# Three small first reads on ACT's queue, transposes of x in another order, and a new order of work in a gated mix of attention and a gated MLP

## The chip, the cores and the metric

The kernel runs on one core of a Trainium2 chip. The metric is the time of one execution on the device, in microseconds (us). TensorE (PE) multiplies matrices, VectorE (DVE), ScalarE (ACT) and GpSimd (POOL) do the rest, and SyncE (SP) issues the DMAs.

## The reference

The input x has 2048 tokens of 512 elements in bf16. Two branches are computed from it and mixed by a gate per token.

```python
x = A_x
g = _sigmoid((x * gate_w).sum(-1, keepdims=True))
a = _A_ref(x, A_wq, A_wk, A_wv, A_wo, A_beta)     # attention
b = _B_ref(x, B_W_gate, B_W_up, B_W_down)         # gated MLP, F = 1792
return g * a + (1 - g) * b
```

`_A_ref` has 32 heads of 16 elements and cuts the tokens into 4 segments of 512. Within a segment it is causal softmax attention. Beside it, each segment reads a memory `M` (with its norm `z`) that sums `phi(k) v` over the segments before, and a gate per head mixes the two. `_B_ref` is `(relu(x Wg) * (x Wu)) Wd`.

## The kernel before, in words

Everything is held in SBUF. A segment passes through these stages: projections to q, k and v (lines 770 to 814), scores in 18 "visits" (`att`, L872; the score matmuls are L904), the exponential of a visit in one pass over four PSUM banks by ACT (L920), masks of the diagonal by POOL (L926), the product with V (L960), a read-out of the memory (L847), an update of the memory (L827), the MLP's first half by 14 column blocks (L1034, with relu on ACT or DVE at L1042 and L1043, and the product with the up branch on DVE at L1045), and its second half together with the output projection (L1066, L1073). Results go through `osb` to DRAM (L1085).

The first segment's x is read in two halves into `hT` (L627) and transposed by PE against an identity (L700) into four PSUM banks, in two halves h and four quarters kt. DVE and ACT copy the results into `xT` in turns (L705). The weights follow on SP's queue in the order of the calls of `load`: wq, wk, wv, the first halves of the gate (wg) and up (wu) weights, the gate vector, beta (`braw`), and the second halves (L617). The x of later segments is read by transposing DMAs (L619). ek, from which the memory is updated, is transposed by DMA too (`phik`, L807). Rows of x for the token gate go through `osb` (L734, L737).

The order of the work isn't written by hand. `Sched` (L129) is a planner that runs while the program is built: each operation has a cost in ns, what it reads and writes, and a queue with a priority. Step by step the planner takes the operation that can start first (`_choose`, L462), gives it a PSUM bank, and appends it to its engine's list with the semaphore waits that it needs (`_waits`, L359). It has tables of how long DMAs take (`DCOST`, L35, and `LAND0`, L36). Where several operations are ready, random numbers decide; their seeds are listed by stretches of 8 us (L565). Thus a change of a cost or a seed at one place shifts the order of everything behind it. At the end SP waits for each DMA's semaphore (L1157).

The waits for several semaphores are sorted by name:

```python
for st, idx in sorted(deps.items(), key=lambda kv: (kv[0] == e, kv[0])):
```

Of the kernel before, what the change touches and what calls it, by code (L numbers as in the profile page):

```python
# [8 lines left out]
ACT = mybir.ActivationFunctionType  # L9
ALU = mybir.AluOpType  # L10
# [21 lines left out]
X2_T = 34000.0  # L32
H1_T = 14000.0
LX = 300.0
DCOST = {"ldbraw": 1800.0, "ldgwb": 1300.0, "ldx1_0": 1500.0, "vsh0": 1100.0, "vsh1": 1100.0, "vsh2": 1100.0, "vsh3": 1100.0}  # L35
# [8 lines left out]
ADP = 1  # L44
# [84 lines left out]
class Sched:  # L129
# [3 lines left out]
    def __init__(self, ndma=16, nbanks=8, seeds=(0,)):  # L133
        self.seeds = seeds
        self.jit = {}
        self.knobs = {}
        self.low_from = False
        self.mates = ()
        self.bank_ep = [None] * nbanks
        self.ndma = ndma  # L140
        self.streams = list(self.ENGS) + [f"dma{i}" for i in range(ndma)]
        self.cnt = {s: 0 for s in self.streams}
        self.know = {e: {s: 0 for s in self.streams} for e in self.ENGS}
        self.snap = {s: {0: {t: 0 for t in self.streams}} for s in self.streams}
# [12 lines left out]
        self.prog = {e: [] for e in self.ENGS}  # L157
        self.busy = {e: 0.0 for e in self.ENGS}
        self.ops = []
        self.log = []  # L160
        self.sem = {}
# [207 lines left out]

    def place(self, op, e, start):  # L370
        op.eng = e
        if op.ep is not None and op.role == "w" and op.ep.bank is None:
            got = self._banks(op, e)[0]
            for ep, bi in zip([g[0] for g in got], sorted(g[1] for g in got) if op.ep.cls == "main" else [g[1] for g in got]):
                for i in range(bi, bi + ep.nb):
                    if self.bank_ep[i] is not None:
                        op.preds += [(r, False) for r in self.bank_ep[i].readers]
                    self.bank_ep[i] = ep
                ep.bank = bi
        if e == "pool" and self.yield_to is not None:  # L380
            op.preds.append((self.yield_to, False))
            self.yield_to = None
        deps = {}
        for p in self._pred_done(op, e):
            deps[p.stream] = max(deps.get(p.stream, 0), p.idx)
        self._waits(e, deps)
        occ = op.occs[e]
        op.base = occ
        if e == "dve" and op.port:
            if self.pool_from <= start < self.now["pool"]:  # L390
                occ += self.now["pool"] - start
                self.yield_to = op
            self.port_free = start + occ
        if e == "pool":
            if start > self.now["pool"] + 1.0:
                self.pool_from = start
        if e == "pe":
            if op.mode != self.mode or start > self.now[e] + 60.0:
                occ += SWITCH
            self.mode = op.mode  # L400
        if op.dma:
            d = min(range(self.ndma), key=lambda i: (self.dma_end.get(i, 0.0), i))
            st = f"dma{d}"
            if self.cnt[st] > 0:
                self._waits(e, {st: self.cnt[st]})
            self.cnt[st] += 1
            self.semval[st, self.cnt[st]] = self.semval.get((st, self.cnt[st] - 1), 0) + 16 * op.nd
            inc = 16
            issued = start + occ
            op.end = max(self.dma_busy + self.dcost(op) if op.nbytes > 4096 and op.name not in LAND0 else 0.0, start + self.landing(op, start) + (0.0 if op.name in LAND0 else LX))  # L410
            self.dma_busy = max(self.dma_busy, op.end) if op.nbytes > 4096 else self.dma_busy
            self.dma_end[d] = op.end
        else:
            st = e
            self.cnt[st] += 1
            inc = 1
# [12 lines left out]
        self.busy[e] += occ  # L429
        self.log.append((start, start + occ, e, op.name))  # L430
# [128 lines left out]
def build_kernel(nc, A_x, A_wq, A_wk, A_wv, A_wo, A_beta, W_g, W_u, W_d, gate_w, out):  # L559
# [5 lines left out]
    sc = Sched(seeds=(140892, 423927, 0, 0, 0, 892626, 168011, 223314, 641091, 969207, 0, 695128, 872014, 0, 136527, 629242, 695393, 450067, 491946, 378858, 0, 909379, 857173, 62279, 0, 744487, 417792, 0,))  # L565
    T = {}
    with contextlib.ExitStack() as stack:
        for name, shape, dt in plan(S, D, F):
# [10 lines left out]
def program(sc, nc, T, PS, A_x, A_wq, A_wk, A_wv, A_wo, A_beta, W_g, W_u, W_d, gate_w, out, NSEG, KT, NF, NT, EPS, SCALE):  # L579
# [19 lines left out]
    def act(fn, occ, **k):  # L599
        return op("act", fn, occ, **k)  # L600
# [41 lines left out]
    load("sp", ["braw"], V.braw[:], A_beta.partition_broadcast(128), 8192)  # L642
    load_gu(1)
    lact.insert(0, act(lambda e: e.activation(V.eb[:, 0:8], nc.const_aps.tensor(1.0, [128, 8], BF16), ACT.Exp), 1450, writes=["eb"], name="tab"))
    sc.queue(0, lact)
    sc.queue(0, lsp)
    lsp = []
# [17 lines left out]
    st = []  # L665
# [25 lines left out]
        return pe(fn, m * n * (0.834 if k == 0 else 0.5), writes=[f"bankL{b}"], name=f"warm{k}")  # L691

    xps, xcs = [warm(5, 512, 0, 3), warm(6, 128, 0, 3)], {"dve": [], "act": []}
    for h in range(2):
        for kt in range(KT):
            eng = ("dve", "act")[kt % 2]

            def fx(e, h=h, kt=kt):
                for i in range(2):
                    ins = e.matmul(PL[:, kt, 128 * i:128 * i + 128], lhsT=V.hT[:, 2 * h + i, kt * 128:(kt + 1) * 128], rhs=V.ident[:], start=True, stop=True)  # L700
                return ins
            xps.append(pe(fx, 205, reads=[f"hT{2 * h}", "ident"], writes=[f"bankL{kt}"], name=f"xt{4 * h + kt}"))
            src = PL[:, kt, 0:256].rearrange("q (i t) -> q t i", i=2)
            dst = V.xT[:, kt, h * 256:(h + 1) * 256].rearrange("q (t i) -> q t i", i=2)
            cpy = (lambda e, d=dst, x=src: e.tensor_copy(d, x)) if eng == "dve" else (lambda e, d=dst, x=src: e.activation(d, x, ACT.Copy))  # L705
            xcs[eng].append(op(eng, cpy, 440 if eng == "dve" else 400, reads=[f"bankL{kt}"], writes=[f"xT0_{kt + 4 * h}"], name=f"xc{4 * h + kt}"))
    sc.queue(0, xps)
    sc.queue(0, xcs["dve"])
    sc.queue(0, xcs["act"])
# [162 lines left out]
    def att(s, between):  # L872
# [57 lines left out]
        def flush():  # L930
# [52 lines left out]
            ds.append((dve if s == NSEG - 1 or not ADP else pool)(lambda e: e.tensor_tensor(av, Tv[:, :, :, 0:16], gv.unsqueeze(3).to_broadcast([128, 2, 16, 16]), ALU.mult), 690 if s == NSEG - 1 or not ADP else 1100, reads=tn + [f"rdg{G % 2}"], writes=["adT"], name=f"ad{s}_{G}"))  # L983
# [210 lines left out]
```

## Time and profile before

| what | us |
|---|---|
| runs | 265.81, 265.82, 266.25 (median 265.82) |
| profiled execution, own time | 266.2 |
| its span in the trace | 264.5 |
| mean granted clock of PE | 0.999 |

The profile is of one execution. The page gives each engine's busy time as a share of the span, then the span in 40 slices with the busy share in tenths, and the chain of work that ended last. The other views group instructions by line, list who waited for whom, or list instructions in order of time; "x4" is the count that was merged into a row, and the bracket at the end of a row is the idle time before it and what ended it. "PEld" is the load of weights into PE, which overlaps its matmuls. "SPq" is SP issuing a DMA; its duration is that of the issue, not of the transfer. Numbers such as L904 are lines of the kernel before; in the kernel after the same line stands 2 to 9 lines further down.

### The profile page before, as it was taken

What the parts mean: (1) busy time and instruction counts of PE and PEld (TensorE: products, weight loads), DVE (VectorE), ACT (ScalarE), POOL (GpSimd) and SP (SyncE); (2) the same over time, 40 slices, a digit from 0 to 9 for tenths busy, and PEclk for the clock granted to TensorE, in tenths of its full rate; (3) what the DMA queues carried; (4) which work ended last, traced back from release to release, by engine and by line L of the source; (5) the groups of instructions that cost most, each with busy time, mean ns of one, the idle gap of its engine ahead of it and who ended that gap; (6) DMA issues with size and microseconds to landing.
All of it is one profiled execution on the core that took longest, in us unless ns stands there. A gap on an engine that the chain in (4) does not pass through costs nothing.

```text
span 264.5 us, 6437 instructions
## 1 busy us (share of the span) xinstructions
PE 255.7 (97%) x2618; PEld 114.0 (43%) x2653; DVE 179.8 (68%) x355; ACT 185.5 (70%) x161; POOL 130.8 (49%) x295
## 2 busy tenths in 40 slices
PE   8899999999999999999999999999999999999996
PEld 4333443434444444434443544434444444344444
DVE  5378597888788494688788775776664676557600
ACT  4577688987788877876868676886786565676021
POOL 3026565645655464865556375756464454544000
PEclk9999999999999999999999999999999999999999
DMA  6889744912550223210141112500132100000011
GB/s 203 268 318 225 147 100 89 296 38 56 85 126 9 58 60 85 59 22 2 40 107 41 42 40 44 62 19 4 33 89 64 42 0 22 21 2 0 2 42 40
DMA packets 34829, 19.87 MB, mean 75 GB/s; under 512 B 23920, under 2 KB 34032, under 8 KB 34800
## 3 DMA queue, kind: packets, MB, share of 16 engines
q1 hardware_dynamic: 34800, 19.46, 30.2%
q8 instruction: 21, 0.34, 0.5%
q14 instruction: 8, 0.07, 0.1%
HBM read 10.40 MB, written 2.11 MB: 47 GB/s over the span
## 4 chain that ended last, share of the span: by engine, by line
PE 91%; SPq 3%; DMA 2%; issue 2%; DVE 1%; DVEq 0%
PE ps L1034 37%; PE ps L1073 19%; PE ps L904 9%; PE ps L784 8%; PE ps L960 7%; PE ps L782 5%; PE ps L1066 5%; SPq L617 3%; DMA wu<-in_B_W_up_dram 2%; PE ps L847 1%; PE ps L827 0%; DVE Tn L970 0%; DVE qT L793 0%; DVE oT L986 0%; DVE osb L1082 0%
## 5 line engine op out<-in xcount | busy, mean ns | idle before, releaser
L926 POOL TENSOR_SCALAR_AFFINE_SELECT E<-E 64x256 bf16<-64x256 bf16 (+1 forms) x256 | 111.0, 444 | 109.6 <-ACT E L920 83.9
L920 ACT ACTIVATE E<-ps 128x2048 bf16<-128x2048 f32 x72 | 135.0, 1875 | 36.8 <-PE ps L904 36.3
L1034 PE MATMUL ps<-xT,wg 128*128 128x512 bf16 x215 | 58.1, 380 | 2.4 <-DMA wg<-in_B_W_gate_dram 1.4
L1034 PE MATMUL ps<-xT,wu 128*128 128x512 bf16 x215 | 57.2, 380 | 1.3 <-issue 1.0
L1073 PE MATMUL ps<-wd,hT 128*128 128x512 bf16 (+2 forms) x229 | 54.0, 367 | 1.1 <-issue 0.9
L1045 DVE TENSOR_TENSOR hT<-ps,rl 128x512 bf16<-128x512 f32 x56 | 38.4, 686 | 19.4 <-PE ps L1034 19.0
L1034 PEld LDWEIGHTS ps<-xT,wg 128*128 128x128 bf16 x224 | 20.3, 98 | 27.7 <-issue 3.9
L1034 PEld LDWEIGHTS ps<-xT,wu 128*128 128x128 bf16 x224 | 20.1, 98 | 25.9 <-issue 2.7
L1073 PEld LDWEIGHTS ps<-wd,hT 128*128 128x128 bf16 x238 | 21.1, 98 | 23.0 <-issue 2.8
L970 DVE STREAM_TRANSPOSE Tn<-ps 128x512 f32<-128x512 f32 x32 | 21.2, 695 | 13.9 <-PE ps L960 13.9
L904 PE MATMUL ps<-qT,kp 32*128 32x192 bf16 (+7 forms) x512 | 28.6, 287 | 0.0
L1043 DVE TENSOR_SCALAR rl<-ps 128x512 bf16<-128x512 f32 x31 | 21.2, 684 | 5.0 <-PE ps L1034 4.2
L1042 ACT ACTIVATE rl<-ps 128x512 bf16<-128x512 f32 x25 | 14.9, 598 | 13.1 <-PE ps L1034 13.1
L904 PEld LDWEIGHTS ps<-qT,kp 32*128 32x128 bf16 x512 | 8.3, 92 | 25.5 <-issue 13.1
L960 PE MATMUL ps<-E,vaug 64*17 64x128 bf16 (+7 forms) x512 | 18.7, 284 | 0.0
L960 PE MATMUL ps<-E,vsh 64*17 64x128 bf16 (+7 forms) x512 | 18.3, 283 | 0.0
L1083 ACT ACTIVATE osb<-ps,omg 128x512 bf16<-128x512 f32 (+1 forms) x9 | 6.1, 675 | 16.9 <-PE ps L1066 14.0
L784 PE MATMUL ps<-xT,wq 128*128 128x512 bf16 x64 | 16.5, 380 | 0.1
L1082 DVE TENSOR_SCALAR osb<-ps,omg 128x512 bf16<-128x512 f32 (+1 forms) x8 | 5.6, 699 | 16.0 <-PE ps L1066 11.4
L1066 PE MATMUL ps<-wo,oT 128*128 128x512 bf16 (+2 forms) x66 | 16.4, 367 | 0.1
L784 PE MATMUL ps<-xT,wk 128*128 128x512 bf16 x60 | 15.9, 380 | 0.3 <-issue 0.2
L782 PE MATMUL ps<-wv,xT 128*128 128x512 bf16 x62 | 15.4, 380 | 0.2 <-issue 0.2
(68 smaller groups left out, 229.9 us busy)
## 6 DMA issues: line engine op xcount, KB each, us to landing
vsh<-vaug SPq DMA_DIRECT2D x8, 272.0 KB, 3.7
osb<-in_A_x_dram SPq DMA_DIRECT2D x16, 128.0 KB, 2.3
out_dram<-osb SPq DMA_DIRECT2D x15, 128.0 KB, 1.7
wg<-in_B_W_gate_dram SPq DMA_DIRECT2D x8, 224.0 KB, 5.9
wu<-in_B_W_up_dram SPq DMA_DIRECT2D x8, 224.0 KB, 6.1
wd<-in_B_W_down_dram SPq DMA_DIRECT2D x1, 1792.0 KB, 10.3
hT<-in_A_x_dram SPq DMA_DIRECT2D x2, 256.0 KB, 3.0
wq<-in_A_wq_dram SPq DMA_DIRECT2D x4, 128.0 KB, 3.0
```

The lines of the kernel that those rows point to most:

```text
L782: ins = e.matmul(A(ep)[:, :], lhsT=V.xT[:, kt, tok + col * 128:tok + (col + 1) * 128], rhs=w[:, kt, :], start=(kt == 0), stop=(kt == KT - 1))
L784: ins = e.matmul(A(ep)[:, :], lhsT=w[:, kt, col * 128:(col + 1) * 128], rhs=V.xT[:, kt, tok:tok + 512], start=(kt == 0), stop=(kt == KT - 1))
L904: ins = q.matmul(dst, lhsT=V.kp[r, kslot(s, G), c, :], rhs=V.qT[r, qslot(s, G), q0:q0 + w], start=True, stop=True, tile_position=(32 * jj, ...
L920: acts.append(act(lambda a: a.activation(V.E[:, base * 512:base * 512 + min(2048, 4 * W)], PF[:, 0:min(2048, 4 * W)], ACT.Exp, scale=SCALE ...
L926: pools.append(pool(lambda g, ap=ap, lim=lim, pat=pat: g.affine_select(out=ap, in_=ap, compare_op=ALU.is_ge, fill=0.0, base=lim, pattern=[ ...
L960: ins = q.matmul(A(eps[p])[32 * jj:32 * jj + 17, 64 * (c + u):64 * (c + u + n)], lhsT=v[:, 8 * G + 2 * jj + p, :], rhs=V.E[r, f:f + 64 * n ...
L970: ds.append(dve(lambda e, p=p, ep=eps[p]: e.transpose(V.Tn[:, 2 * (G % (TNN // 2)) + p, :], A(ep)[:, :]), t_dve(512), writes=[f"Tn{2 * (G ...
L1034: ins = e.matmul(A(ep)[:, :], lhsT=w[:, kt, f * 128:(f + 1) * 128], rhs=V.xT[:, kt, c % XR * 512:(c % XR + 1) * 512], start=(kt == 0), sto ...
L1043: ("dve", lambda e, ep=eg, r=r: e.tensor_scalar(V.rl[:, r, :], A(ep)[:, :], 0.0, None, ALU.max), t_dve(512))],
L1045: evs.append(dve(lambda e, ep=eu, r=r, hs=hs: e.tensor_tensor(V.hT[:, hs, :], A(ep)[:, :], V.rl[:, r, :], ALU.mult), t_dve(512), reads=[f" ...
L1066: ins = e.matmul(A(ep)[:, 0:c1 - c0], lhsT=V.oT[:, ot[G], i * 128:(i + 1) * 128], rhs=V.wo[:, G, c0:c1], start=st_ and G == 0, stop=sp_ an ...
L1073: ins = e.matmul(A(ep)[:, 0:c1 - c0], lhsT=V.hT[:, slots[f], i * 128:(i + 1) * 128], rhs=V.wd[:, f, c0:c1], start=st_ and f == f0, stop=sp ...
```

## The change

Three reads of 16 x 32 elements, one each from the gate, up and down weights, are issued on ACT's DMA queue, behind ACT's first exponential (the one that loads its table). They write into `adT`, which holds nothing yet; its first real writer waits for them. No result uses what they read.

The transposes of x have another order, and one of the eight uses a fifth PSUM bank that the planner picks. DVE and ACT still copy four results each, but not the same ones: DVE has (h, kt) = (0,0), (1,0), (0,3), (1,2), ACT has (0,1), (0,2), (1,1), (1,3). Before, DVE had the even quarters and ACT the odd ones, first of h = 0 and then of h = 1.

The planner gets a cost of 1000 ns for the first gate weight's DMA, 10 ns less for each copy of x, and other seeds. With that the whole order of work is planned anew. Waits for several semaphores are listed with the latest first, and so are SP's waits at the end. In the built program PE starts with 16 query matmuls, 14 of the keys, a visit, 2 of the keys, 10 of V, a visit, 6 of V, and then 4 of the gate and 4 of the up weights. Before, the 17th and later matmuls were 10 of the keys, 2 of the gate, 2 of the keys, a visit, and then gate, key, up and V matmuls by turns of two.

```diff
-DCOST = {"ldbraw": 1800.0, ...}
+DCOST = {"ldwg0_0": 1000.0, "ldbraw": 1800.0, ...}
@@ Sched._waits
-        for st, idx in sorted(deps.items(), key=lambda kv: (kv[0] == e, kv[0])):
+        for st, idx in sorted(deps.items(), key=lambda kv: (-self.end_of.get(kv, 0.0), kv[0])):
@@ Sched.place
+        self.end_of[st, idx] = op.end
@@ build_kernel
-    sc = Sched(seeds=(140892, 423927, 0, 0, 0, 892626, ...))
+    sc = Sched(seeds=(237719, 74891, 0, 89398, 0, 53401, ...))
@@ program
     lact.insert(0, act(lambda e: e.activation(V.eb[:, 0:8], ..., ACT.Exp), 1450, writes=["eb"], name="tab"))
+    for n, w in enumerate((W_g, W_u, W_d)):
+        load("act", [f"touch{n}"], V.adT[0:16, 32 * n:32 * n + 32], w[0:16, 0:32], 1024)
...
-    for h in range(2):
-        for kt in range(KT):
-            eng = ("dve", "act")[kt % 2]
+    for h, kt, bank, eng in ((0, 0, 0, "dve"), (0, 1, 1, "act"), (0, 2, 2, "act"), (1, 0, None, "dve"), (0, 3, 3, "dve"), (1, 1, 0, "act"), (1, 2, 1, "dve"), (1, 3, 2, "act")):
+        ep = Epoch("att") if bank is None else None
...
-            xcs[eng].append(op(eng, cpy, 440 if eng == "dve" else 400, ...))
+        xcs[eng].append(op(eng, cpy, 430 if eng == "dve" else 390, ...))
@@ flush, the first writer of adT
-... writes=["adT"], name=f"ad{s}_{G}"))
+... writes=["adT"] + ([f"touch{n}" for n in range(3)] if s + G == 0 else []), name=f"ad{s}_{G}"))
@@ end of program
-    for i in sorted(range(sc.ndma), key=lambda i: sc.dma_end.get(i, 0.0)):
+    for i in sorted(range(sc.ndma), key=lambda i: -sc.dma_end.get(i, 0.0)):
```

More of the change, by code (lines that the diff above doesn't have):

```diff
@@ L34 @@
 LX = 300.0
-DCOST = {"ldbraw": 1800.0, "ldgwb": 1300.0, "ldx1_0": 1500.0, "vsh0": 1100.0, "vsh1": 1100.0, "vsh2": 1100.0, "vsh3": 1100.0}
+DCOST = {"ldwg0_0": 1000.0, "ldbraw": 1800.0, "ldgwb": 1300.0, "ldx1_0": 1500.0, "vsh0": 1100.0, "vsh1": 1100.0, "vsh2": 1100.0, "vsh3": 1100.0}
 LAND0 = {"ldhT0": 2850.0, "ldhT2": 3100.0, "ldwq0": 3150.0, "ldwq1": 3200.0, "ldwq2": 3100.0, "ldwq3": 3000.0}
@@ L157, in __init__ @@
         self.prog = {e: [] for e in self.ENGS}
+        self.end_of = {}
         self.busy = {e: 0.0 for e in self.ENGS}
@@ L564, in build_kernel @@
     EPS, SCALE = 1e-6, 16 ** -0.5
-    sc = Sched(seeds=(140892, 423927, 0, 0, 0, 892626, 168011, 223314, 641091, 969207, 0, 695128, 872014, 0, 136527, 629242, 695393, 450067, 491946, 378858, 0, 909379, 857173, 62279, 0, 744487, 417792, 0,))
+    sc = Sched(seeds=(237719, 74891, 0, 89398, 0, 53401, 416309, 0, 0, 0, 710933, 0, 718714, 120896, 538430, 820480, 585027, 870794, 793690, 0, 589972, 0, 0, 0, 454998, 16783, 0,))
     T = {}
@@ L693, in program, with B, fx, cpy @@
     xps, xcs = [warm(5, 512, 0, 3), warm(6, 128, 0, 3)], {"dve": [], "act": []}
-    for h in range(2):
-        for kt in range(KT):
-            eng = ("dve", "act")[kt % 2]
[L698 to L706, printed above, removed]
+    for h, kt, bank, eng in ((0, 0, 0, "dve"), (0, 1, 1, "act"), (0, 2, 2, "act"), (1, 0, None, "dve"), (0, 3, 3, "dve"), (1, 1, 0, "act"), (1, 2, 1, "dve"), (1, 3, 2, "act")):
+        ep = Epoch("att") if bank is None else None
+        bk = [] if bank is None else [f"bankL{bank}"]
+        def B(ep=ep, bank=bank):
+            return A(ep) if bank is None else PL[:, bank, :]
+        def fx(e, h=h, kt=kt, B=B):
+            for i in range(2):
+                ins = e.matmul(B()[:, 128 * i:128 * i + 128], lhsT=V.hT[:, 2 * h + i, kt * 128:(kt + 1) * 128], rhs=V.ident[:], start=True, stop=True)
+            return ins
+        xps.append(pe(fx, 205, reads=[f"hT{2 * h}", "ident"], writes=bk, name=f"xt{4 * h + kt}", ep=ep, role=ep and "w"))
+        dst = V.xT[:, kt, h * 256:(h + 1) * 256].rearrange("q (t i) -> q t i", i=2)
+        def cpy(e, d=dst, B=B, eng=eng):
+            x = B()[:, 0:256].rearrange("q (i t) -> q t i", i=2)
+            return e.tensor_copy(d, x) if eng == "dve" else e.activation(d, x, ACT.Copy)
+        xcs[eng].append(op(eng, cpy, 430 if eng == "dve" else 390, reads=bk, writes=[f"xT0_{kt + 4 * h}"], name=f"xc{4 * h + kt}", ep=ep, role=ep and "r"))
     sc.queue(0, xps)
@@ L982, in flush @@
             av = V.adT[:, :].rearrange("q (c p e) -> q p c e", p=2, e=16)
-            ds.append((dve if s == NSEG - 1 or not ADP else pool)(lambda e: e.tensor_tensor(av, Tv[:, :, :, 0:16], gv.unsqueeze(3).to_broadcast([128, 2, 16, 16]), ALU.mult), 690 if s == NSEG - 1 or not ADP else 1100, reads=tn + [f"rdg{G % 2}"], writes=["adT"], name=f"ad{s}_{G}"))
+            ds.append((dve if s == NSEG - 1 or not ADP else pool)(lambda e: e.tensor_tensor(av, Tv[:, :, :, 0:16], gv.unsqueeze(3).to_broadcast([128, 2, 16, 16]), ALU.mult), 690 if s == NSEG - 1 or not ADP else 1100, reads=tn + [f"rdg{G % 2}"], writes=["adT"] + ([f"touch{n}" for n in range(3)] if s + G == 0 else []), name=f"ad{s}_{G}"))
             os_ = (s * 4 + G) % OTN
```

## The prediction

> **What bounds the kernel now.** I read the page first: the span, the busy time of TensorE (PE), its row of 40 slices, and the chain that ended last.
>
> ```profile
> span 264.5 us, 6437 instructions
> PE 255.7 (97%) x2618; PEld 114.0 (43%) x2653; DVE 179.8 (68%) x355; ACT 185.5 (70%) x161; POOL 130.8 (49%) x295
> PE   8899999999999999999999999999999999999996
> PE 91%; SPq 3%; DMA 2%; issue 2%; DVE 1%; DVEq 0%
> ```
>
> PE is busy nearly all the time and is 91% of the chain. No other engine passes 70%. The only slices below 9 are the first two and the last. So the second step is the view of busy time in stretches, and the waits of PE.
>
> ```profile
> 5.60:17.40 11.80, 10.19 (x53) 4.00 (x54) 5.72 (x14) 6.47 (x9) 1.34 (x2) 1.00 0.84 276
> 17.50:261.00 243.50, 239.71 (x2527) 106.49 (x2558) 170.25 (x333) 175.71 (x147) 127.11 (x279) 1.00 0.28 63
> PE ps L1034 <- DMA wg<-in_B_W_gate_dram: 1.4, 2, 1.2
> PE ps L1034 <- DMA wu<-in_B_W_up_dram: 0.2, 1, 0.2
> ```
>
> After the length of each stretch, the first number is PE's busy time; 1.00 is the granted clock. From 17.5 us on PE is busy 239.71 of 243.50 us, at full clock, and waits for no transfer. Its only waits for data are in the first stretch: three for the gate and up weights. The third step is the order in time there, and a piece of the middle as a yardstick.
>
> ```profile
> 5.60 3.61 PE L784 MATMUL ps<-xT,wq 128*128 128x512 bf16 x16
> 12.54 0.59 PE L1034 MATMUL ps<-xT,wg 128*128 128x512 bf16 x2 [1.17 <-DMA wg<-in_B_W_gate_dram]
> 13.50 0.39 PE L904 MATMUL ps<-qT,kp 32*128 32x512 bf16 x4
> 14.09 0.59 PE L1034 MATMUL ps<-xT,wg 128*128 128x512 bf16 x2 [0.20 <-DMA wg<-in_B_W_gate_dram]
> 15.31 0.59 PE L1034 MATMUL ps<-xT,wu 128*128 128x512 bf16 x2 [0.19 <-DMA wu<-in_B_W_up_dram]
> 16.60 0.59 PE L1034 MATMUL ps<-xT,wu 128*128 128x512 bf16 x2
> 42.58 0.60 PE L1034 MATMUL ps<-xT,wg 128*128 128x512 bf16 x2
> 43.11 0.40 PE L904 MATMUL ps<-qT,kp 32*128 32x512 bf16 x4
> 43.44 0.61 PE L1034 MATMUL ps<-xT,wg 128*128 128x512 bf16 x2
> 43.88 1.03 PE L1034 MATMUL ps<-xT,wu 128*128 128x512 bf16 x4
> 44.74 1.03 PE L1034 MATMUL ps<-xT,wg 128*128 128x512 bf16 x4
> ```
>
> Starts, not ends, tell PE's pace, since a matmul's recorded length overlaps the next. Four matmuls of 512 columns go from 43.88 to 44.74: **0.216 us each**. A visit to the scores (L904) costs 0.33 us (43.11 to 43.44) and 0.10 to enter it (42.58 plus two steps is 43.01; it starts at 43.11).
>
> With that yardstick the start is measured. Before the first visit stand 30 matmuls of 512 columns (16 for queries, 12 for keys, 2 for the gate): 5.60 + 30 x 0.216 + 0.10 = 12.18. The visit starts at 13.50, so 1.32 us are lost. It ends at 13.83, and the next matmul starts at 14.09: 0.26 lost. Four matmuls later it would be 14.95; the next starts at 15.31: 0.36 lost. Together **1.94 us**, all of it PE waiting for gate and up weights that were put among the keys.
>
> **The change part by part.**
>
> *The order of PE's work.* The instructions of both kernels hold the same work: 946 matmuls of 512 columns or less behind the transposes, 72 visits, 16 products with V, 3 memory updates, 12 read-outs of the memory. PE enters the other kinds of work about as often (78 stretches of plain matmuls against 80, and each visit, product and update follows its kind of neighbour nearly as often), so I put the steady part at no change, 0.0. What moves is the beginning. The new order is 16 query matmuls, 14 of the keys, the first visit, 2 of the keys, 10 of V, the second visit, 6 of V, and only then the gate and up weights. So the 1.94 us of waiting go if what is late next comes in time. Each neighbour by its time, with queries starting at 5.35 (next part): the first visit is due at 5.35 + 6.48 + 0.10 = 11.93. It needs two key tiles copied by ACT and two masks by DVE.
>
> ```profile
> 10.98 0.60 ACT L789 ACTIVATE kT<-ps 128x512 bf16<-128x512 f32 x1 [0.27 <-PE ps L784]
> 11.61 1.06 ACT L766 ACTIVATE ek<-kT 128x1024 bf16<-128x1024 bf16 x1
> 13.94 1.88 ACT L920 ACTIVATE E<-ps 128x2048 bf16<-128x2048 f32 x1 [1.28 <-PE ps L904]
> ```
>
> The second copy ends at 11.58 now, and 0.25 earlier then: 11.33, so 0.6 us of room. The first exponential starts once the visit is through and the 1.06 us pass of ek is done: 12.4 to 14.3. The second visit needs it, and is due at 11.93 + 0.33 + 12 x 0.216 + 0.10 = 14.95: again 0.6. The gate weights are due at 14.95 + 0.33 + 6 x 0.216 = 16.6. The rows above show them landed by 14.09 (both pairs are used by then). The up weights are due at 17.4 and were landed by 16.60. So the whole 1.94 is counted as gained.
>
> *The transposes of x.* Now DVE and ACT copy four results each.
>
> ```profile
> 3.71 1.80 PE L700 MATMUL ps<-ident,hT 128*128 128x128 bf16 x16
> 4.14 1.66 DVE L705 CAST xT<-ps 128x256 bf16<-128x256 f32 x4 [0.98 <-PE ps L700]
> 4.35 1.57 ACT L705 ACTIVATE xT<-ps 128x256 bf16<-128x256 f32 x4 [2.04 <-PE ps L700]
> 5.05 0.46 PE L700 MATMUL ps<-ident,hT 128*128 128x128 bf16 x4
> ```
>
> The first query matmul needs both halves of the first quarter of x. The second half is DVE's third copy: 4.14 + 3 x 0.415 = 5.39, and PE starts at 5.60. In the new order it is DVE's second copy, done by about 5.2. Then the end of the transposes decides. The last one waits for ACT's second copy in both orders (4.35 + 2 x 0.39 = 5.14). Now the last four matmuls start at 5.05 and end at 5.50; at 0.22 each the last starts at 5.28, and a step of 128 columns (a quarter of 0.216) later PE is free: 5.34. So queries start at about 5.35: **0.25 us gained**. From below it is 0, if another copy is late; from above 0.35.
>
> *The three small reads.* ACT issues them after its first exponential and before its copies of x.
>
> ```profile
> 2.10 0.21 ACT L644 ACTIVATE eb<-const-bfloat16-1.0 128x8 f32<-128x8 bf16 x1
> L617 SPq DMA_DIRECT2D wu<-in_B_W_up_dram x8: 430/526/1192, 9.3 to 17.2; - x8
> DMA packets 236, 0.17 MB, mean 145 GB/s; under 512 B 109, under 2 KB 236, under 8 KB 236
> q1 hardware_dynamic: 236, 0.17, 49.4%
> ```
>
> No DMA is issued on ACT now, so its price is bounded by SP's rows: 0.43 to 1.19 us each. ACT is free at 2.31 and needed at 4.35. Three at 0.43 end at 3.6 and cost nothing; three at 1.19 end at 5.9 and delay the start by 1.5. I take 0.43, the usual row while the queue is not full, so 0. What waits behind them on ACT are the copies of x. Their packets are small; the last two rows are the 1.2 us from 15.4 on, when 64-byte packets of another load pass: 236 packets take 49.4% of 16 engines, 40 ns each. Three packets and as many completions per engine are 0.25 us at most for the first query weights, which are not due before 5.35. What the reads may gain is less time for the first gate read; nothing waits for it any more, so 0.
>
> The Trainium skill speaks against these reads (DMA: Bandwidth & Descriptors, "Issuing engines are not separate DMA queues"): DMAs of ACT and SP share 16 engines and interleave, so another issuing engine only saves issue time. By that rule the reads push into the loads of x and query weights; by the 40 ns above that is at most 0.25, and the sum would be 0.25 smaller, an estimate. No run here shows the mix yet.
>
> *Waits listed with the latest first, and the last waits on SP.*
>
> ```profile
> 261.72 1.15 SPq L1085 DMA_DIRECT2D out_dram<-osb  x2
> out_dram<-osb SPq DMA_DIRECT2D x15, 128.0 KB, 1.7
> ```
>
> The last store is issued near 262.5 and lands 1.4 to 1.7 later, so 264.0 to 264.2; the span ends at 264.5. At most 0.5 lies behind the landing. In the built program the wait for that store moves from the second to last place on SP to the last, so one wait less is left behind it. Bounds 0 to 0.4; I take 0, as only one of some ten steps moves. Elsewhere PE, which sets the time, hardly waits, so the order of waits is worth 0 there.
>
> **Sum.** 1.94 + 0.25 = 2.19 us. The profiled execution's own time is 266.2 (span 264.5 and 1.7 around it): 264.0. It stands 0.4 above the median of the runs, 265.82; from that the sum gives **263.65, I say 263.7**.
>
> **The rivals.**
>
> *A. ACT is late.* The three issues take over 0.68 us each (2.04 of room by three), or their packets hold up x. Against it: SP's first issues of 0.43. For it: a queue that has not been used. At 0.9 each the start slips 0.7, at 1.19 by 1.5: 264.3 to 265.2.
>
> *B. Waits come back in small pieces.* The gate and up work starts 4 us later, so DVE meets V copies and key masks together near 14 to 20 us, and a shifted order can put an exponential in front of a visit. One such wait is at most one exponential, 1.88: 264.3 to 265.5. Against it: in the old order nothing of the kind shows in 243.5 us, and visits in the new order are no closer to each other (2.6 us at the least in both, by the prices above).
>
> *C. Slower: x of the second segment is behind on SP.* Now three of its four transposed pieces are issued by 25.4 us, the fourth at 30.54.
>
> ```profile
> 22.97 2.45 SPq L619 DMA_TRANSPOSE xT<-in_A_x_dram  x2
> 26.82 3.68 SPq L807 DMA_TRANSPOSE phik<-ek  x2
> 30.54 1.26 SPq L619 DMA_TRANSPOSE xT<-in_A_x_dram  x1
> 31.85 3.03 SPq L734 DMA_DIRECT2D osb<-in_A_x_dram  x3
> DMA to landing us min/median/max: 2.7/3.1/4.8
> 33.94 1.03 PE L784 MATMUL ps<-xT,wq 128*128 128x512 bf16 x4
> 24.76 0.90 DVE L768 TENSOR_TENSOR ek<-ek,ttmp 128x1024 bf16<-128x1024 bf16 x1
> ```
>
> In the new order three of them stand behind the transposes of ek and two loads of rows of x, one of which waits for a gate pass on DVE. From the second ek pass (done at 25.66 now) I count 2 x 1.26, 2 x 0.6 and 2 x 1.25 until the last issue starts at 31.9; with 2.7 to 3.1 to land (the row of landings) it is in at 34.6 to 35.0. PE wants it at 33.94 - 2.19 + 16 matmuls + one visit = 35.6. So 0.6 to 1.0 of room, and each us beyond it stops PE one for one. To end slower than 266.35 it must be 0.6 + 2.2 + 0.5 = 3.3 us late, one full round of waiting on DVE; then 266.4 to 268.
>
> *D. The reads do not do what they are named for.* If the first gate reads are as slow as now, nothing changes here: 263.7 as well.
>
> **How the numbers follow.** A difference under 0.2% (0.53 us) can't be told from no change here. Forecast, D within it: 0.68, at 263.2 to 264.3. A: 0.12. B: 0.14, a third of it within 0.2%. C: 0.06. Faster (under 265.29): 0.68 + 0.11 + 0.08 = 0.87; same 0.06; slower 0.07. The range goes from 263.2 to 265.0: the forecast with its bounds (start gain 0.35; last waits 0.4), and most of A and B.
>
> **What would show it.** In the changed kernel's timeline the queries start at 5.3 to 5.4; the first visit at 11.9 to 12.0 and the second at 15.0; no wait of PE for the gate or up weights; three issues on ACT that end before 4.3; the query work of segment two near 35.6 with no wait for x; and a span of about 262.3. I am wrong if PE shows gaps between 12 and 40 us, or if ACT's first copy starts after 4.4.

## The result, and the profile after

| | runs | median, us | lowest to highest |
|---|---|---|---|
| before | 6 | 266.13 | 265.81 to 266.30 |
| changed | 6 | 264.32 | 263.60 to 264.61 |

The ratio is 0.9931, with a 95% interval of 0.9915 to 0.9946: 1.81 us faster, where 2.19 were forecast. The forecast of 263.7 started from the median of the first three runs, 265.82; that of all six is 266.13. 264.32 lies at the upper edge of the forecast's own 263.2 to 264.3, and at the lower edge of what rivals A and B were given. The profiled execution of the changed kernel took 264.5 us, 1.7 less than that of the kernel before.

The page of the changed kernel (span, busy time, PE's 40 slices, the chain that ended last):

```profile
span 262.7 us, 6432 instructions
PE 255.7 (97%) x2619; PEld 114.6 (44%) x2653; DVE 179.1 (68%) x356; ACT 184.5 (70%) x160; POOL 131.0 (50%) x295
PE   8999999999999999999999999999999999999996
PE 97%; issue 1%; DVE 1%
```

PE is busy for the same 255.7 us in a shorter span, and the two 8s at the start have become one. DMA and SP are gone from the chain. The waits of PE in the changed kernel, the longest first:

```profile
PE ps L1043 <- issue: 1.6, 10, 0.2
PE ps L693 <- PEq L1188: 0.8, 1, 0.8
PE ps L793 <- issue: 0.6, 4, 0.2
PE ps L1082 <- issue: 0.6, 4, 0.2
PE ps L1043 <- DVE Tn L979: 0.2, 1, 0.2
```

No row names the gate or up weights. (L1043 is the line that was L1034, L793 was L784 and L913 was L904.) The start of the changed kernel in order of time:

```profile
3.69 1.95 PE L707 MATMUL ps<-ident,hT 128*128 128x128 bf16 x16
5.43 4.21 PE L793 MATMUL ps<-xT,wq 128*128 128x512 bf16 x16
9.48 3.19 PE L793 MATMUL ps<-xT,wk 128*128 128x512 bf16 x13
12.60 0.40 PE L913 MATMUL ps<-qT,kp 32*128 32x512 bf16 x4
13.37 2.32 PE L791 MATMUL ps<-wv,xT 128*128 128x512 bf16 x10
15.62 0.40 PE L913 MATMUL ps<-qT,kp 32*128 32x448 bf16 x8
17.26 1.03 PE L1043 MATMUL ps<-xT,wg 128*128 128x512 bf16 x4
```

From the first visit at 12.60 on, the rows follow the prices: the second visit stands 0.33 + 12 x 0.216 + 0.10 = 3.02 later. But the first visit was forecast for 11.93. The second row tells why: 16 query matmuls take 4.21 us where they took 3.61. Up to the first key they take 9.48 - 5.43 = 4.05, against 9.05 - 5.60 = 3.45. The 0.60 more is what about 1.2 us at half the pace cost: until about 6.6 us a matmul took 0.43, then 0.216. The trace also holds a record of the granted clock, and its first entry, at full clock, begins at 6.63. The transposes of x (first row) stand ahead of that and ran at half pace too.

The difference of the spans (264.45 to 262.75 in the trace, 1.71) then splits as follows: the two stretches of waiting 1.32 + 0.60; the earlier start of the queries 0.17; the slow first queries -0.59; steps elsewhere 0.06; the end, behind the last matmul, 0.15.

### The profile page after: what moved, and what is told of

Same layout as the page of the kernel before. It is cut to its first block, busy times and chain, and to the rows that moved or that the text cites. A ratio compares the mean times of both kernels' runs of the same rounds, so it can differ in the third digit from the quotient of the medians.

```text
span 262.7 us, 6432 instructions
## 1 busy us (share of the span) xinstructions
PE 255.7 (97%) x2619; PEld 114.6 (44%) x2653; DVE 179.1 (68%) x356; ACT 184.5 (70%) x160; POOL 131.0 (50%) x295
## 4 chain that ended last, share of the span: by engine, by line
PE 97%; issue 1%; DVE 1%
PE ps L1043 38%; PE ps L1082 19%; PE ps L793 11%; PE ps L913 9%; PE ps L969 6%; PE ps L791 5%; PE ps L1075 5%; PE ps L856 1%; PE ps L693 1%; PE ps L707 1%; PE ps L836 0%; DVE hT L1054 0%; DVE Tn L979 0%; DVE osb L746 0%; DVE osb L1091 0%
## 5 line engine op out<-in xcount | busy, mean ns | idle before, releaser
L1043 PE MATMUL ps<-xT,wu 128*128 128x512 bf16 x213 | 57.2, 380 | 1.4 <-issue 1.3
L1043 PE MATMUL ps<-xT,wg 128*128 128x512 bf16 x219 | 57.7, 380 | 0.6 <-issue 0.3
L1082 PE MATMUL ps<-wd,hT 128*128 128x512 bf16 (+2 forms) x229 | 52.8, 367 | 0.9 <-issue 0.6
L1043 PEld LDWEIGHTS ps<-xT,wg 128*128 128x128 bf16 x224 | 20.6, 98 | 25.7 <-issue 2.8
L1043 PEld LDWEIGHTS ps<-xT,wu 128*128 128x128 bf16 x224 | 20.1, 98 | 25.4 <-issue 3.5
L913 PE MATMUL ps<-qT,kp 32*128 32x192 bf16 (+7 forms) x512 | 28.6, 287 | 0.0
L1051 ACT ACTIVATE rl<-ps 128x512 bf16<-128x512 f32 x26 | 15.5, 598 | 9.9 <-PE ps L1043 9.7
L913 PEld LDWEIGHTS ps<-qT,kp 32*128 32x128 bf16 x512 | 8.2, 92 | 25.3 <-issue 13.1
L793 PE MATMUL ps<-xT,wq 128*128 128x512 bf16 x61 | 16.1, 391 | 0.4 <-issue 0.3
L793 PE MATMUL ps<-xT,wk 128*128 128x512 bf16 x60 | 15.6, 380 | 0.4 <-issue 0.3
```

What stands on the lines that cost most here:

```text
L793: ins = e.matmul(A(ep)[:, :], lhsT=w[:, kt, col * 128:(col + 1) * 128], rhs=V.xT[:, kt, tok:tok + 512], start=(kt == 0), stop=(kt == KT - 1))
L913: ins = q.matmul(dst, lhsT=V.kp[r, kslot(s, G), c, :], rhs=V.qT[r, qslot(s, G), q0:q0 + w], start=True, stop=True, tile_position=(32 * jj, ...
L1043: ins = e.matmul(A(ep)[:, :], lhsT=w[:, kt, f * 128:(f + 1) * 128], rhs=V.xT[:, kt, c % XR * 512:(c % XR + 1) * 512], start=(kt == 0), sto ...
L1082: ins = e.matmul(A(ep)[:, 0:c1 - c0], lhsT=V.hT[:, slots[f], i * 128:(i + 1) * 128], rhs=V.wd[:, f, c0:c1], start=st_ and f == f0, stop=sp ...
```

## The experiments

*Changed* is the kernel after. The experiments ran in three groups of four (1 to 4, 5 to 8, 9 to 12), each beside the kernel before on the same chip, which had medians of 266.52, 266.19 and 266.43. Ratios are to it. The most telling numbers of all traces stand in one table (us):

| kernel | queries from | 16 queries take | first visit | span |
|---|---|---|---|---|
| before | 5.60 | 3.45 | 13.50 | 264.5 |
| before, short warm-up | 5.70 | 4.22 | 13.52 | 264.6 |
| before, reads alone | 6.00 | 3.46 | 13.25 | 264.4 |
| before, new transposes | 5.19 | 3.46 | 13.06 | 267.0 |
| before, gate late by cost | 5.47 | 3.45 | 12.04 | 268.8 |
| before, gate late by hand | 5.58 | 3.48 | 11.75 | 264.9 |
| before, all but reads and middle | 5.41 | 3.45 | 11.54 | 265.7 |
| changed | 5.43 | 4.05 | 12.60 | 262.7 |
| changed, second time | 5.27 | 3.45 | 11.84 | 262.0 |
| changed, third time | 5.53 | 3.45 | 12.10 | 262.9 |
| changed, no reads | 5.51 | 3.45 | 12.08 | 262.2 |
| changed, old waits | 5.42 | 3.94 | 12.48 | 262.8 |
| changed, old transposes | 5.60 | 3.45 | 12.16 | 263.4 |
| changed, short warm-up | 5.44 | 5.41 | 13.96 | 264.1 |

**1. The changed kernel a second time.** No edit.

> The changed kernel once more, unchanged, for a second profile. Theory (the time at which PE gets its full clock is a matter of chance, since the clock is granted at the ends of windows that run freely): the granted clock turns full at another time than 6.6 us, somewhere from 4.3 to 7.7, and the first visit moves with it between 11.9 and 13.0. Rival (the new order of the transposes holds the clock back): it turns at 6.6 again within 0.1. Time 1.5 to 2.0 us below before in both.

Measured: 263.90 us, ratio 0.9902 (0.9881 to 0.9924). Its start:

```profile
5.27 3.61 PE L793 MATMUL ps<-xT,wq 128*128 128x512 bf16 x16
8.72 3.18 PE L793 MATMUL ps<-xT,wk 128*128 128x512 bf16 x13
11.84 0.39 PE L913 MATMUL ps<-qT,kp 32*128 32x512 bf16 x4
```

The same instructions have full pace from the first query, and the visit stands at 5.27 + 30 x 0.216 + 0.10 = 11.85. So the slow queries come and go from run to run; the new transposes aren't their cause. The record of the clock begins at full at 3.81 here, sooner than the 4.3 that was expected at the least. Twelve of the fourteen traces hold such a record, and in each the matmuls ahead of its first entry run at half pace and those behind it at full pace. It begins at 4.76 in the kernel before, among the transposes, and at 9.39 in the changed kernel with a short warm-up, among the queries. Without slow queries this trace's span is 2.47 below before: 1.92 of waiting, 0.33 by queries that start sooner, 0.15 at the end and 0.07 elsewhere.

**2. The changed kernel without the three reads.** They are taken out after planning, so that no other instruction moves.

```diff
+        sc.drop(["ldtouch0", "ldtouch1", "ldtouch2"])
```

> The changed kernel without the three small reads, all other instructions in the same order. Theory (the gain is PE's order; nothing waits for the first gate read any more): within 0.3 us of the changed kernel, and no wait of PE for gate or up weights. Rival (the reads make the gate and up weights land in time): 1.3 to 1.9 us slower, with PE waiting for the gate weights near 17 us.

Measured: 264.24 us, ratio 0.9912 (0.9891 to 0.9933), the same as with them within the intervals. PE waits for no gate or up weight without them either.

**3. The changed kernel with the old order of waits.** Same instructions, each group of waits sorted by name again, and SP's last waits the old way round.

```diff
+                if item is None and e == "sp":
+                    run.reverse()
+                else:
+                    run.sort(key=lambda w: (w[1] == e, w[1]))
```

> The changed kernel with the same instructions in the same order, but the waits of each instruction sorted by name and SP's last waits in the old order. Theory (one wait less behind the last store, and the last copy of DVE starts 0.10 sooner): 0.15 to 0.25 us slower. Rival (the order of waits is worth nothing): within 0.1.

Measured: 264.62 us, ratio 0.9932 (0.9910 to 0.9953). Most of its 0.7 us over the second run of the changed kernel (0.79 between the two traces) is the first visit at 12.48 instead of 11.84, slow queries again. The rest is at the end. The last matmul starts at 260.12 and DVE's last copy at 260.45, 0.33 later (0.26 in all seven traces of kernels with the new waits, 0.36 in the six others with the old). Behind the landing of the last store the span goes on for 0.48, as in those six, against 0.42 or less in the seven. So latest-first waits are worth 0.07 to 0.10 at the last copy and 0.06 behind the last store.

**4. The kernel before, gate work later by a cost.** One number makes its planner expect the gate weights late; all the order behind is planned anew.

```diff
-DCOST = {"ldbraw": 1800.0, ...}
+DCOST = {"ldwg0_0": 4000.0, "ldbraw": 1800.0, ...}
```

> The kernel before with one number added: the planner takes 4000 ns for the first gate weight's DMA, so it puts 14 of the keys before the first visit, and 8 V matmuls before the first gate matmul. No small reads, old transposes, old order of waits. Theory (PE's order alone takes away 1.94 us of waiting): 1.5 to 2.0 us faster than before, first visit near 12.2, no wait of PE for gate or up weights. Rival (the reads are needed): 0 to 0.3 faster, with waits for the weights still there.

Measured: 271.07 us, ratio 1.0164 (1.0127 to 1.0200): slower, though the start went as wanted (first visit 12.04, second 15.06, no wait for gate or up weights). The waits of PE, and PE's busy time in four stretches of its trace (length, PE, PEld, DVE, ACT, POOL, granted clock, DMA share, GB/s):

```profile
PE ps L904 <- ACT E L920: 1.8, 4, 0.8
PE ps L1066 <- DVE oT L986: 1.3, 1, 1.3
```

```profile
85.90:89.30 3.40, 2.85 (x22) 1.13 (x20) 2.03 (x6) 3.39 (x3) 2.23 (x6) 1.00 0.93 202
89.30:92.70 3.40, 1.32 (x8) 0.61 (x10) 3.01 (x8) 3.40 (x4) 1.98 (x5) 1.00 0.46 103
92.70:96.10 3.40, 3.40 (x16) 0.87 (x14) 1.74 (x3) 2.77 (x2) 2.09 (x3) 0.50 0.20 52
96.10:99.50 3.40, 3.32 (x110) 1.99 (x110) 2.85 (x6) 1.75 (x1) 0.92 (x2) 1.00 0.15 43
```

Exponentials that are late for a visit, rival B's mechanism, cost 1.8 us, a late copy of the attention's result 1.3. Between 89.3 and 92.7 PE is busy only 1.32 of 3.40 us, and for the next 3.4 us the granted clock is 0.50: another 1.7 us. (Five of the six executions have a mean clock of 0.994 and took 270.51 to 272.61; the one at 1.000 took 268.86, 1.65 less than the profiled one.) These 4.8 us are more than twice what the start could gain. An early start is worth nothing if the rest doesn't follow.

**5. The kernel before with the reads alone**, issued on ACT behind its table load; the rest in the old order.

```diff
+                        if op.name == "tab":
+                            for fn in self.extra:
+                                fn(engobj).then_inc(self.sem["touch"], 16)
```

> The kernel before with the three small reads alone, issued on ACT right behind its table load; every other instruction in its old order. My theory, that the reads are not what the change gains by: PE's first gate matmul waits 1.17 us in the kernel before, and the first gate weights landed 0.47 us sooner in the changed kernel, so the wait shrinks by 0 to 0.5 us and the two later ones (0.2 each) take some of it back: ratio 0.998 to 1.000. Rival 1, the reads are the change: the waits of PE for gate and up weights go, ratio 0.993. Rival 2, the reads push the query weights back (0.4 us in the changed kernel for the first two) and this shows: queries start later than 5.75 and the ratio is 1.001 to 1.002.

Measured: 266.59 us, ratio 1.0014 (0.9997 to 1.0031). The start:

```profile
6.00 3.63 PE L792 MATMUL ps<-xT,wq 128*128 128x512 bf16 x16 [0.27 <-DVE xT L713]
14.01 0.59 PE L1042 MATMUL ps<-xT,wg 128*128 128x512 bf16 x2 [0.36 <-DMA wg<-in_B_W_gate_dram]
15.26 0.59 PE L1042 MATMUL ps<-xT,wu 128*128 128x512 bf16 x2 [0.23 <-DMA wu<-in_B_W_up_dram]
```

The waits stay. The first query weights landed at 5.95 here and the queries start just behind. Queries behind 5.75 and a ratio of 1.001 to 1.002 are what rival 2 named, and the theory's 0.998 to 1.000 was missed. But one trace doesn't put this down to the reads: these weights landed at 4.78 to 5.95 in the seven traces with reads (mean 5.31) and at 4.46 to 5.37 in the seven without (mean 5.08). A small push by the reads is neither shown nor excluded. The first visit is 0.25 earlier than before, and the second 0.05 (17.08 against 17.13): the next weight's wait took it back. The reads alone gain nothing.

**6. The kernel before with the new transposes alone.** Its planner lays out the rest again.

```diff
-    for h in range(2):
-        for kt in range(KT):
-            eng = ("dve", "act")[kt % 2]
+    for h, kt, bank, eng in ((0, 0, 0, "dve"), (0, 1, 1, "act"), (0, 2, 2, "act"), (1, 0, None, "dve"), ...):
```

> The kernel before with the new order of the transposes and copies of x alone; its planner lays the rest out again, and starts with 16 query, 12 key and 2 gate matmuls as before. My theory: queries start 0.1 to 0.25 us sooner than 5.60, and the wait for the gate weights grows by as much, since these land by their own time (11.8): ratio 1.000 for the start, and whatever its new middle adds, which shows as waits of PE in the trace (the kernel before with another order of work had 3.1 us of them). Rival: the transposes are worth their 0.2 us by themselves, ratio 0.999 with no new waits.

Measured: 268.53 us, ratio 1.0081 (1.0063 to 1.0099).

```profile
5.19 3.63 PE L789 MATMUL ps<-xT,wq 128*128 128x512 bf16 x16 [0.21 <-DMA wq<-in_A_wq_dram]
12.53 0.59 PE L1039 MATMUL ps<-xT,wg 128*128 128x512 bf16 x2 [1.13 <-DMA wg<-in_B_W_gate_dram]
```

Queries start 0.41 sooner, and the gate's matmul starts at 12.53 as before (12.54): the wait for the weights took it all, as expected. The new middle again has waits of its own (0.8 for an exponential, 0.6 for a transfer of phik, 0.4 for DVE).

**7 and 8. Both kernels with a short warm-up**: two matmuls of 64 columns on constants in place of eleven. Their results are used by nothing.

```diff
-            for i in range(m):
-                ins = e.matmul(PL[:, b, 0:n], ...)
+            for i in range(1):
+                ins = e.matmul(PL[:, b, 0:64], ...)
```

> The changed kernel with its warm-up matmuls cut to two of 64 columns (their results are used by nothing), all other instructions in their order. Theory, a late clock is paid in full: the granted clock turns to full some 3 us after the first transposes or later (6.9 to 10), the queries that run before it take 0.43 us instead of 0.216, and the span grows by half of the time between 5.4 and the turn: 0.7 to 2.3 us more than the unchanged kernel with an early turn, no wait further on that takes it back. Rival: the start has slack elsewhere (first visit due at 12, its masks and copies of keys ready later), then under 0.4 us.

> The kernel before with the same cut of the warm-up. Theory, the wait for the gate weights takes up a late clock: the wait of 1.17 us shrinks by what the queries lose, so the span grows by 1.3 to 1.9 us less than in the changed kernel with the same cut, between 0 and 0.8 us against the kernel before; ratio 1.000 to 1.003. Rival: a late clock costs both kernels the same, 0.7 to 2.3 us, ratio 1.003 to 1.009, and the spread of the changed kernel has another cause.

Measured: changed 265.82 us (264.15 to 267.23), ratio 0.9973 (0.9950 to 0.9996); before 266.76 us (265.85 to 266.99), ratio 1.0011 (0.9997 to 1.0026). The start of the changed kernel with it, and then of the kernel before with it:

```profile
5.44 5.57 PE L793 MATMUL ps<-xT,wq 128*128 128x512 bf16 x16
10.85 3.18 PE L793 MATMUL ps<-xT,wk 128*128 128x512 bf16 x14
13.96 0.39 PE L913 MATMUL ps<-qT,kp 32*128 32x512 bf16 x4
```

```profile
5.70 4.38 PE L784 MATMUL ps<-xT,wq 128*128 128x512 bf16 x16
9.92 2.32 PE L784 MATMUL ps<-xT,wk 128*128 128x512 bf16 x10
13.52 0.39 PE L904 MATMUL ps<-qT,kp 32*128 32x512 bf16 x4
14.50 0.38 PE L1034 MATMUL ps<-xT,wg 128*128 128x512 bf16 x1 [0.58 <-DMA wg<-in_B_W_gate_dram]
```

In the changed kernel the queries take 5.41 us, the first visit is 2.12 late, and every later visit with it: spans 264.1 against 262.0. In the kernel before they take 4.22, and its first visit stands at 13.52 against 13.50: the wait for the gate weights took up the late pace, and 0.17 of it is left from the second visit on. The two had not the same to bear: the record of the clock turns to full at 9.39 in the first trace and at 7.28 in the second, which cost their queries 1.96 and 0.77. The spreads point the same way, 3.1 us in the changed kernel and 1.1 in the kernel before; but with its full warm-up the kernel before spread over 2.4 us in its 29 runs beside them, so this is a hint only. By the traces, then, the wait that the change removes had been a cover, for a cost that comes by chance.

**9. The kernel before, gate work later by hand.** Its own order is written out, and only four pairs of gate and up matmuls move behind the second visit (with DVE's two passes over their result); eight matmuls of V stand between the visits instead.

```diff
-... k0_2, wg0_0, k0_2, quad0_0_0, wg0_0, k0_3, wu0_0, k0_3, v0_0, wu0_0, quad0_0_1, wg0_1, v0_0, v0_1, v0_1, ...
+... k0_2, k0_2, quad0_0_0, k0_3, k0_3, v0_0, v0_0, v0_1, v0_1, quad0_0_1, wg0_0, wg0_0, wu0_0, wu0_0, wg0_1, ...
```

> The kernel before with its own order of work written out, and one thing moved: the four pairs of gate and up matmuls that stood among the keys come behind the second visit (eight matmuls of V take their place between the visits), and on DVE the two passes over their result stand behind the copies of V; no reads, old transposes, old order of waits. My theory, that this alone is the gain: the first visit is due at 5.60 + 28 x 0.216 + 0.10 = 11.75 with an early clock and the third at 18.7 instead of 20.58, PE no longer waits for gate or up weights, and the time falls by 1.9 less what a late clock costs (0 to 0.8): ratio 0.993 to 0.995. Rival: the wait is replaced by one for DVE or ACT behind the second visit, as in the other new order of the kernel before (3.1 us of waits): ratio 0.999 or more.

Measured: 267.58 us (266.44 to 271.11), ratio 1.0025 (1.0000 to 1.0051). The rival won, though not where I had put it:

```profile
11.75 0.40 PE L904 MATMUL ps<-qT,kp 32*128 32x512 bf16 x4
19.08 0.40 PE L904 MATMUL ps<-qT,kp 32*128 32x384 bf16 x8
33.75 1.04 PE L784 MATMUL ps<-xT,wq 128*128 128x512 bf16 x4 [1.15 <-DMA xT<-in_A_x_dram]
```

The first visit is at 11.75 to the hundredth, the third 1.50 sooner than before. (One pair of up matmuls still waits for its weights, 0.26 us at 16.83.) Then the queries of the second segment wait for its x, and start at 33.75; before it was 33.94. Of 1.50 us 0.19 are left. The last of that x's four transposing DMAs, issue to landing, first in the kernel before (issued at 30.54), then here (29.49):

```profile
xT<-in_A_x_dram SPq DMA_TRANSPOSE x1, 2.7
```

```profile
xT<-in_A_x_dram SPq DMA_TRANSPOSE x1, 4.2
```

Before, it landed at 33.19, 0.75 ahead of PE. Here it was issued 1.05 sooner, and with the flight of before it would have landed at 32.14, ahead of PE, which comes for it at 32.60 and waits 1.15. So the gain went with the longer flight. Another 0.6 us went near 195 us, in a wait of PE for DVE: the planner picked other PSUM banks for some results when the order was written out. The profiled execution (266.59) is among the quickest of this kernel. Three of the twelve have a lower mean clock (0.994, 0.987, 0.987) and took 269.39 to 271.11; the nine at 1.000 took 266.44 to 267.96, and what makes most of these slower than the profiled one no trace shows.

**10. That kernel with the new transposes and the latest-first waits**, so with everything but the reads and the new middle.

> The kernel before with the late gate and up pairs, the new transposes and the waits listed latest first; no reads, and the middle of the old plan. Theory: it does all that the change does for the time, so it stands within 0.3 us of the changed kernel (263.9 to 264.5), ratio 0.992. Rival: the reads or the new middle are worth something, and it stays 0.4 us or more behind.

Measured: 269.13 us, ratio 1.0083 (1.0052 to 1.0114). The rival holds, and by experiments 2 and 5 it isn't the reads: the new middle is worth more than all the rest. Here another transfer is late:

```profile
33.95 0.70 PE L834 MATMUL ps<-vaug,phik 128*64 128x68 bf16 x32 [2.33 <-DMA phik<-ek]
```

The visits stand 1.85 us ahead of the kernel before until 28 us and 1.41 behind it from 34.58 on. The profiled execution (267.45) is a quick one: the three with a mean clock of 1.000 took 266.94 to 267.45, and the nine with 0.987 to 0.994 took 268.94 to 270.61. Stretches at half clock like the one of experiment 4 would fit that, as PE does nothing from 31.6 to 33.95 here; no trace shows such an execution. Even the three at full clock are 2.7 us behind the changed kernel.

The changed kernel issues the four transposes of ek ahead of x (all landed at 29.62, PE uses them at 32.61) and puts 12 gate and up matmuls and a visit in front of the second segment's queries.

**11. The changed kernel with the old transposes**, all other instructions in their order (written out, too).

> The changed kernel with the old order of the transposes and of the copies of x, all other instructions of all engines in their order. Theory: between the landing of the second half of x and the first query matmul lie 1.25 to 1.4 us instead of 1.0 to 1.2, so the time is 0.2 us over the unchanged one that runs beside it: ratio 0.993 against 0.992. Rival: the copies are not what the queries wait for, no difference in that distance.

**12. The changed kernel a third time**, beside it.

> The changed kernel once more, beside the others: 263.6 to 264.6, by when the clock turns; ratio 0.992. Between the first query and the first visit lie 6.58 us with an early clock and up to 0.8 more with a late one.

Measured: 265.34 us, ratio 0.9955 (0.9935 to 0.9976), with the old transposes; 264.28, ratio 0.9902 (0.9874 to 0.9929), without an edit. The 1.06 between them can't be put down to the transposes. The rows of the kernel with the old ones:

```profile
5.60 3.61 PE L793 MATMUL ps<-xT,wq 128*128 128x512 bf16 x16
150.77 0.43 PE L856 MATMUL ps<-Mbd,phiq 128*128 128x136 bf16 x4 [0.46 <-DVE hT L1054]
168.03 0.43 PE L856 MATMUL ps<-Mbd,phiq 128*128 128x136 bf16 x4 [0.35 <-DVE rl L1052]
```

Two waits at 151 and 168 us, 0.52 and 0.53 on the visits behind them, come from other PSUM banks, as in 9; they add up to 1.05. At the start this pair shows no step, as the rival has it: the queries begin 1.24 us after the second half of x landed, 1.23 in the third run of the changed kernel and 1.16 in the second; over all traces of both orders it is 0.99 to 1.38 with the new transposes (mean 1.18, eight traces) and 1.24 to 1.46 with the old (mean 1.35, five; the one of experiment 5, where the weights were late, is left out). So the step is worth about 0.2 by these means, whose ranges overlap; no pair of runs shows it by itself.

The third run of the changed kernel holds one more line:

```profile
36.42 1.04 PE L793 MATMUL ps<-xT,wq 128*128 128x512 bf16 x4 [0.48 <-DVE gl L746]
```

DVE had been done long before; the last piece of the second segment's x landed at 36.37. That is rival C: 0.48 us of idle time, and 0.66 on the visits behind it against the second run.

## Why the prediction was right, and where it was off

**What bounds the kernel, and the yardstick.** Right. The 0.216, 0.33 and 0.10 gave the first visit to 0.02 us in experiments 1 and 9.

**The 1.94 us of waiting.** Right: 1.92 are gone, in every trace of the changed order. What the step left out is what the wait covered. It counted a wait as a loss whose place nothing takes, and checked four neighbours in the first 18 us. A late clock had lived under it too, and cost 0.59 here. The second segment's transfers lived under it as well, 0.75 us ahead of PE. These the prediction did weigh, as rival C, with the queries moved back by 16 matmuls and a visit; experiment 9, whose queries aren't moved back, lost its gain there.

**The steady part at no change.** Right for this order, within 0.06 us, but by luck as far as the argument goes. It counted the same work and as many switches between kinds of work. The orders of experiments 4 and 6 hold the same work as well, and are 4.6 and 2.3 us slower than the kernel before. What this order does better shows only as waits that it doesn't have; no run gives a rule for it.

**The transposes.** The step put queries at 5.35 and gained 0.25; they start at 5.43 (0.17), and between 5.19 and 5.53 in other traces with the new transposes. What failed is "the first query weights are not due before 5.35". In six of these eight traces they land at 5.13 to 5.39, and the queries start 0.05 to 0.14 us behind: the weights are late next. The execution with 5.43 isn't among the six, as its weights landed at 5.09. There the late clock held the transposes: the last starts at 5.33, and the queries one step at half pace (0.11) behind it, where the step took 5.28 and 0.054.

**The reads.** The cost of 0 was right, the place wrong. ACT in the changed kernel:

```profile
0.81 1.28 ACT L646 ACT_TABLE_LOAD   x1 [0.81 <-PEq L1188]
0.87 0.39 ACTq L619 DMA_DIRECT2D adT<-in_B_W_gate_dram  x1
1.77 0.44 ACTq L619 DMA_DIRECT2D adT<-in_B_W_down_dram  x1
4.34 0.66 ACT L714 ACTIVATE xT<-ps 128x256 bf16<-128x256 f32 x2 [2.03 <-PE ps L707]
```

They are issued beside the table load from 0.87 to 2.21, not behind the exponential at 2.10, at the 0.43 that was taken. The first copy of x stands at 4.34 (4.35 before). What they may gain was put at 0, and experiments 2 and 5 confirm it. Whether rival D was true is open, and makes no difference to the time: the first gate weights landed at 11.32 to 11.69 in the seven traces with reads and at 11.37 to 12.29 in the seven without. The rule of the Trainium skill (DMA: Bandwidth & Descriptors, "Issuing engines are not separate DMA queues") agrees in that a second issuing engine gained nothing; the 0.25 that the prediction took for it lies within the scatter of the landings.

**The order of waits.** Taken as 0, bounds 0 to 0.4: 0.15 by experiment 3 and the split of the spans.

**The sum.** 2.19 forecast; 0.59 less for the clock, 0.08 less for the transposes, 0.15 more at the end, and 0.04 of small terms: 1.71 in the profiled execution. The term that was missing is the clock. In the profile of before the 16 queries had full pace, and I took that for granted. How late it turns is chance: with full pace (experiment 1) the same sum comes to 2.47, above the forecast.

**The rivals.** A did not occur, although the time lies at the edge of its range. B is real in orders planned anew (experiments 4 and 6) and absent in this one. C is real, but smaller than its price here: I had x landed at 34.6 to 35.0 and due at 35.6. It landed at 35.2 to 36.4 in six traces of the changed order, 3.6 to 4.3 after its issue instead of 2.7 to 3.1; PE came 0.15 to 0.7 us later in five of them and had to wait in one. In the kernel of experiment 9 the same mechanism ate the gain.

## What to carry to other kernels

Before a wait is counted as gained, list what lives under it: the pace of the first matmuls, and the next transfers, with their lead over PE (here 0.75 us against a gain of 1.9) and with how far their flight varies (2.7 to 4.2). Then follow the gain through the stages by the starts of one repeated row, such as the visits, until the end; a gain at 12 us that is gone at 34 is no gain. A start that PE alone sets also shows every delay that comes by chance, so it takes several profiles to know it.

## What the runs showed of the hardware

- The pace of PE's first matmuls turns to full at a point that differs between runs of one program: 16 queries took 3.45, 3.45 and 4.05 us in three runs of the changed kernel, whose records of the clock begin at full at 3.81, 5.43 and 6.63. The granted clock's column can't show it: it reads 1.00 from 0.84 us on in five traces (both kernels, the second run, both short warm-ups), the slow queries among them, as it counts the time ahead of the record's first entry as full. In experiment 4, where it does show, the clock was 0.50 for 3.41 us, one window of about 3.4 us after one with PE busy 39%. The Trainium skill (TensorE: Matmul & The Clock Gate, "Part 1: The HAM clock gate") tells of a free-running window of 3413 ns. The trace agrees with that length, 3.41; but the page names an idle window as what brings the half clock back, and the window here was 39% busy.
- The DMA issues on ACT didn't wait for ACT's table load in front of them (0.87 against its end at 2.09).
- In six traces (both kernels, the second and third runs, experiments 9 and 10) the transfers nearly stand still for 0.5 to 1.25 us somewhere between 32.75 and 35.5 us. The stretches of before, then of the changed kernel (granted clock, DMA share and GB/s last):

```profile
34.25:35.50 1.25, 1.25 (x8) 0.54 (x7) 1.16 (x3) 1.25 (x1) 1.25 (x4) 1.00 0.08 17
```

```profile
34.50:35.25 0.75, 0.75 (x10) 0.22 (x9) 0.75 (x2) 0.11 (x1) 0.50 (x2) 1.00 0.07 8
```

Before, this fell behind the landing of the second segment's x (33.19); with the faster start it falls ahead of it (36.04), which fits the longer flight. It doesn't prove it: there are shorter stops elsewhere (2 and 0 GB/s from 31.25 to 31.75 in the kernel before, inside the flight of 2.7), and other transfers are in flight beside the longer ones. A 16 KB read on the instructions' queue stands 1 to 2 us ahead of the stop in all six traces. Whether that read causes it was not tried.
